# A block-sparse attention with two expert layers: four small edits of its first stage, and its hand-drawn order of work drawn up again

## The chip, the cores and the metric
One core of a Trainium2 chip runs the whole program; the other seven have no part in it. Times are device microseconds (us) of one execution. The time before is the median of three runs.

## What is computed
The reference, cut to what matters. Attention with a narrow window, and a summary of each 32 tokens as additional keys and values, then two dense layers:

```python
q, k, v: (2, 8, 768, 64)              # batch, heads, tokens, head width; float32
k_sum = k.reshape(B, H, 24, 32, D).max(axis=3)
v_sum = v.reshape(B, H, 24, 32, D).mean(axis=3)
scores_l = where(|pos_q - pos_k| < 16, scale * q @ k.T, -1e9)
scores_s = scale * q @ k_sum.T + log(32)
a = softmax(concatenate([scores_l, scores_s]))
x = a @ concatenate([v, v_sum])       # (1536 tokens, 512)
h = x @ moe_w_in                      # 512 -> 2048
x = (h * clip(h + 3, 0, 6) / 6) @ moe_w_out
h = x @ moe2_w_in
return (h * sigmoid(h)) @ moe2_w_out
```

## The kernel before, in words
The program is one list of some 1,960 named operations (`ORDER`, from line 111), which is walked through once. An entry is a function of the kernel with its numbers (`tr k 0 1 0` is `transposed("k", 0, 1, 0)`), and a star puts it on VectorE where it has a choice. Every engine takes its own instructions strictly in that order: PE (TensorE), DVE (VectorE), ACT (ScalarE), POOL (GpSimd), and SP (SyncE), on whose one queue all transfers are issued. So an instruction that waits holds up all that its engine has after it. Buffers and PSUM banks come from rings (`Ring`): `take` gives the buffer that has been free longest, `use` counts down its users. The compiled program has a wait wherever a buffer is taken again.

The stages. A batch has three blocks of 256 tokens for each of k, q and v. `load` (L458 and L473) brings a block in: keys of batch 0, and its first query block, as pairs of rows (512 B a piece), which `par` (by_parity, L486) sorts into even and odd tokens, one half on DVE, one on ACT; other k and q blocks come as two transfers with rows of 256 B straight into `raws`, a ring of two buffers in all. `tr` (L500) transposes half a block on PE in four matmuls; `k_copy` (L508) and `k_max` (L514) take keys and their block maxima out of the bank, `q_copy` (L527, L529) the queries. For each of 24 windows of 64 queries (a unit, numbered over both batches, 12 in each), `keys` (L591, L594) copies the 96 near keys and the 24 block maxima side by side; `scores` (L608) multiplies for two units at once, in 32 small matmuls; `masked` (L623) adds the mask and finds the row's maximum on DVE, `exps` (L637) are four exponentials on ACT, followed by `guard` (L648), `inverse` (L652) and `normal` (L657, on POOL or DVE); `turn` (L665) transposes the result and `turned` (L670) copies it out. `v_sums` (L545) sums values over 32 tokens on PE, each of the three blocks in its own bank; `v_add` (L556, L558) adds the three up in `vsum` on DVE, `v_rows` (L564) and `v_put` (L574) lay the sums beside the values that `load_v` (L581) brings per unit. `mix` (L679) multiplies two units with their values; `mixed_hi` and `mixed_lo` (L701, L705) split the result in two parts of reduced precision for the layers.

The layers: `fetch` (L416, L418) brings weights in 511 KB pieces into a ring of three (`words`), `conv_top`, `conv_join`, `conv_hi`, `conv_lo` (L426 to L450) split them into two parts; `hidden` (L721) is the first matmul of a step in 12 matmuls of 512 columns, in two halves, `project` (L798, L801) the second; the later part, from some 200 us on, goes by products of sums (`prod`, `prodb`, L1025). `warm` (L1173) and `rouse` (L1185) are groups of two matmuls on data that nobody uses, put where PE would wait.

## Time and profile before
| | |
|---|---|
| Median of three runs | 585.75 us (585.04 to 585.86) |
| The profiled execution, its own time | 585.98 us |
| Its span, from the first instruction to the last | 584.1 us |
| Mean granted TensorE clock | 1.00 |
| PE, DVE, ACT, POOL busy in the span | 97%, 79%, 46%, 16% |
| Bytes moved | 51.57 MB, mean 88 GB/s |

The shares are means over very different stages. In the first 60 us transfers, attention and the first weights run beside each other; later PE alone is full. A stage is read from its own stretch, and the engine that limits it from what its neighbours wait for. In a chain of waits each line is what ended last; a line of a transfer covers its issue, queueing and landing.

### The profile page before, as it was taken

To read this page: it belongs to the slowest core of one execution; us is meant where nothing else is said; L and a number is where in the kernel's file an instruction comes from. 1 tells how busy PE (TensorE), PEld (TensorE's weight loads), DVE (VectorE), ACT (ScalarE), POOL (GpSimd) and SP (SyncE) were. 2 spreads that over 40 slices of the span, in tenths; PEclk is the share of its full clock that TensorE was granted. 3 is DMA by queue.
4 is the path that set the end of the run, shared out by engine and by line. 5 is a ranking of instruction groups with operands and counts; after the bars stand their busy time and mean duration, and the time that the engine had idled before them with its cause. 6 is when DMAs were issued, how large, how long until landed. Compare 5 with 4: busy or idle time off the path is not lost.

```text
span 584.1 us, 9467 instructions
## 1 busy us (share of the span) xinstructions
PE 566.9 (97%) x3536; PEld 476.7 (82%) x3536; DVE 462.3 (79%) x1012; ACT 269.6 (46%) x626; POOL 95.8 (16%) x111
## 2 busy tenths in 40 slices
PE   6778999999999999999999999999999999999997
PEld 6667788888888788888888888888888898888886
DVE  4899888874776999998999999585877686757764
ACT  4798865542313345541646565545534234424220
POOL 1756252101010012121100202000100000111000
PEclk9999999999999999999999999999999999999999
DMA  9999982323010112333220110223122211210013
GB/s 239 258 191 261 214 202 87 100 64 98 0 38 0 51 57 73 109 89 119 80 71 3 37 37 30 79 77 125 50 73 83 98 37 36 73 66 8 1 71 146
DMA packets 69054, 51.57 MB, mean 88 GB/s; under 512 B 36368, under 2 KB 63504, under 8 KB 69008
## 3 DMA queue, kind: packets, MB, share of 16 engines
...
q14 instruction: 18, 0.15, 0.1%
...
## 4 chain that ended last, share of the span: by engine, by line
PE 88%; DVE 5%; DMA 3%; ACT 2%; issue 1%; SPq 0%; POOL 0%; DVEq 0%
PE bank L1025 29%; PE bank L801 22%; PE bank L798 20%; PE bank L721 11%; PE bank L679 2%; PE bank L665 1%; DMA stage<-in_v_dram 1%; PE bank L608 1%; DMA early_units<-in_v_dram 1%; ACT early_units L637 1%; DVE kmax L514 1%; DMA cst<-in_consts_dram 1%; PE bank L500 1%; DVE w L928 0%; DVE bits L435 0%
## 5 line engine op out<-in xcount | busy, mean ns | idle before, releaser
L801 PE MATMUL bank<-w,g 128*128 128x512 f32 (+1 forms) x477 | 111.7, 385 | 0.0
L798 PE MATMUL bank<-g,w 128*128 128x512 f32 x444 | 108.7, 391 | 0.4 <-DVE g L778 0.4
L801 PEld LDWEIGHTS bank<-w,g 128*128 128x128 f32 x477 | 88.2, 188 | 17.7
L450 POOL TENSOR_TENSOR w<-bits,w 128x512 fp32r<-128x512 f32 x34 | 47.9, 1411 | 304.0 <-ACT w L446 213.5
L798 PEld LDWEIGHTS bank<-g,w 128*128 128x128 f32 x444 | 82.5, 188 | 17.7 <-DVE g L778 0.8
L1025 PE MATMUL bank<-w,x 128*128 128x512 f32 (+1 forms) x360 | 73.9, 348 | 0.5 <-DVE w L971 0.5
L1025 PEld LDWEIGHTS bank<-w,x 128*128 128x128 f32 x360 | 59.4, 189 | 10.0 <-DVE w L971 0.8
L1025 PE MATMUL bank<-x,w 128*128 128x512 f32 (+1 forms) x240 | 49.6, 348 | 0.0
L426 ACT CAST top<-words 128x512 f16<-128x512 bf16 x51 | 39.7, 778 | 19.9 <-DVE bits L435 11.0
L721 PE MATMUL bank<-x,w 128*128 128x512 f32 x192 | 47.7, 396 | 0.0
L435 DVE SCALAR_TENSOR_TENSOR bits<-words,top 128x512 uint32<-128x512 uint32 x47 | 35.6, 756 | 14.0 <-ACT top L426 11.8
L1025 PEld LDWEIGHTS bank<-x,w 128*128 128x128 f32 x240 | 39.1, 189 | 5.5
L721 PEld LDWEIGHTS bank<-x,w 128*128 128x128 f32 x192 | 35.3, 188 | 7.8 <-issue 0.4
L778 DVE TENSOR_TENSOR g<-values,g 128x512 fp32r<-128x512 f32 x46 | 32.6, 712 | 7.4 <-ACT g L772 7.0
L752 ACT ACTIVATE values<-values 128x512 f32<-128x512 f32 x35 | 22.0, 628 | 29.3 <-DVE values L1066 17.0
L798 PE MATMUL bank<-w,w 128*128 128x512 f32 x132 | 33.6, 392 | 0.0
L752 ACT ACTIVATE r<-r 128x512 f32<-128x512 f32 x27 | 17.0, 629 | 28.9 <-DVE r L1072 20.0
L1072 DVE TENSOR_TENSOR values<-bank,values 128x512 f32<-128x512 f32 x39 | 26.5, 687 | 3.1 <-PE bank L1025 2.6
L798 PEld LDWEIGHTS bank<-w,w 128*128 128x128 f32 x132 | 24.5, 188 | 5.1 <-issue 0.2
L450 POOL TENSOR_TENSOR w<-cst,w 128x512 fp32r<-128x512 f32 x10 | 14.2, 1418 | 87.8 <-DVE w L446 60.6
L1025 PE MATMUL bank<-w,w 128*128 128x512 f32 (+1 forms) x144 | 28.1, 337 | 0.0
L772 ACT CAST g<-values 128x512 fp32r<-128x512 f32 x33 | 20.4, 621 | 16.7 <-PE bank L801 6.5
...
## 6 DMA issues: line engine op xcount, KB each, us to landing
...
out_dram<-acc SPq DMA_DIRECT2D x11, 256.0 KB, 2.0
early_w<-in_q_dram SPq DMA_DIRECT2D x10, 256.0 KB, 6.7
...
stage<-in_k_dram SPq DMA_DIRECT2D x3, 512.0 KB, 5.2
early_w<-in_k_dram SPq DMA_DIRECT2D x6, 256.0 KB, 6.2
stage<-in_v_dram SPq DMA_DIRECT2D x3, 512.0 KB, 7.5
```

The source lines that it names most:

```text
L426: copier("conv_top", h)(out=top[:, 1], in_=src[:, 2])
L435: nc.vector.scalar_tensor_tensor(out=bitss.take(h, bit_users(h)), in0=rest, scalar=13, in1=tops.use(h).bitcast(U32), op0=ALU.logical_shift ...
L450: eng.tensor_tensor(out=w_half(h, 1), in0=bitss.use(h).bitcast(F32), in1=w_half(h, 0).bitcast(F32), op=ALU.subtract,)
L679: nc.tensor.matmul(ps[D * e : D * e + D, o : o + QW], v[:NSLOT, h * D : (h + 1) * D], own(pTs, 2 * n + e)[:NSLOT, hp * P + QW * w : hp * P ...
L721: nc.tensor.matmul(ps[:, :n], w[:, a, kk * P : (kk + 1) * P], x[:, o // SUB : (o + n) // SUB, b, kk, :], start=(m == 0), stop=(m == last),)
L752: nc.scalar.activation(out=r, in_=ps, **kind)
L772: copier("gate_hi", i)(out=g[:, 0, cols], in_=value(i)[:, cols])
L778: eng.tensor_tensor(out=g[:, 1, cols], in0=r[:, cols], in1=g[:, 0, cols].bitcast(F32), op=ALU.subtract)
L798: nc.tensor.matmul(ps[:, o : o + n], lhs, g[:, b, shift : shift + n], **flags)
L801: nc.tensor.matmul(ps[:, : len(cols)], g[:, a, rows], rhs, **flags)
L1025: nc.tensor.matmul(ps, lhs(a, kk), rhs(b, kk), start=(i == 0), stop=(i == 5))
L1072: nc.vector.tensor_tensor(out=out, in0=banks.use(("prod", p, k)), in1=r, op=ALU.add)
```

## The change
Four edits in the code, and the first half of the list in another order. The order's last 957 entries are the same in both.

1. The first query block (`load q 0 0`) comes row by row, like the others, into `raws`; its two `par` entries are gone.
2. The value sums of a batch's three blocks accumulate in one bank, and `v_add` is one copy for the batch.
3. `scores 0` (units 0 and 1) reads near keys and maxima in place, in 64 matmuls, and `keys 0` and `keys 1` are gone.
4. There are twelve `rouse` groups where there were six.

In the list, `load v 1 0` goes behind the weights of the first layer steps, the first weights (`fetch 0`) and third query block (`load q 0 2`) behind values, and the first keys of batch 1 forward. Some 110 entries change between DVE and another engine. No work of the layers is added or left out.

```diff
+DIRECT = 1
...
-load k 0 1, zero, table 0, rouse 0, warm 6, load k 0 2, par k 1 0, load k 0 0, par k 1 1, par k 2 1, grow 9,
...
+zero, rouse 2, rouse 10, rouse 5, rouse 7, load k 0 0, par k 0 1, rouse 11, par k 0 0, table 0, clear,
...
-        if b == 0 and (what == "k" or T == 0):
+        if b == 0 and what == "k":
...
+    vdone = [0, 0]
...
-        ps = banks.take(("v", b, T), 1)
+        done = vdone[b]
+        vdone[b] += 1
+        if done == 0:
+            banks.take(("v", b), 1)
+        ps = banks.see(("v", b))
...
-                    start=(r == 0),
-                    stop=(r == 1 - b),
+                    start=(done == 0 and r == 0),
+                    stop=(done == 2 and r == 1 - b),
...
-    def v_add(b, T):
-        ps = banks.use(("v", b, T))
-        if T == 0:
-            nc.vector.tensor_copy(out=vsum, in_=ps[:, :P])
-        else:
-            nc.vector.tensor_tensor(out=vsum, in0=ps[:, :P], in1=vsum, op=ALU.add)
+    def v_add(b):
+        nc.vector.tensor_copy(out=vsum, in_=banks.use(("v", b))[:, :P])
...
-        kw = [own(kws, 2 * n + w) for w in range(2)]
+        if n < DIRECT:
+            near = [key_rows(b)[:, :, (t + w) * QW : (t + w) * QW + LOC] for w in range(2)]
+            pieces = [(0, near), (LOC, [kmax[b]] * 2)]
+        else:
+            pieces = [(0, [own(kws, 2 * n + w) for w in range(2)])]
```

Three places of the order, as the compiled programs have it. First, SP's queue from its start; a row is one transfer (or `x2`), `stage` and `early_w_88` are the buffers of pairs and of single rows, `128x8x128` are pieces of 512 B and `128x8x64` of 256 B. Before:

```order
L458 DMA stage_80<-in_k_dram 128x8x128
L1167 DMA cst<-in_consts_dram 128x176
L458 DMA stage_80<-in_k_dram 128x8x128
L458 DMA stage_81<-in_k_dram 128x8x128
L458 DMA stage_83<-in_q_dram 128x8x128
L473 DMA early_w_88<-in_k_dram 128x8x64 x2
L416 DMA words_69<-in_moe_w_in_dram 128x4x511
L1167 DMA cst<-in_consts_dram 128x360
L473 DMA early_w_88<-in_q_dram 128x8x64 x2
L458 DMA stage_84<-in_v_dram 128x8x128
L473 DMA early_w_88<-in_q_dram 128x8x64 x2
L458 DMA stage_84<-in_v_dram 128x8x128
```

And with the change:

```order
L459 DMA stage_80<-in_k_dram 128x8x128
L1178 DMA cst<-in_consts_dram 128x176
L474 DMA early_w_88<-in_q_dram 128x8x64 x2
L459 DMA stage_81<-in_k_dram 128x8x128
L474 DMA early_w_88<-in_k_dram 128x8x64 x2
L459 DMA stage_82<-in_k_dram 128x8x128
L1178 DMA cst<-in_consts_dram 128x360
L459 DMA stage_83<-in_v_dram 128x8x128 x2
L474 DMA early_w_88<-in_q_dram 128x8x64 x2
L459 DMA stage_84<-in_v_dram 128x8x128
L474 DMA early_w_88<-in_q_dram 128x8x64 x2
L417 DMA words_69<-in_moe_w_in_dram 128x4x511
```

The first queries moved ahead of two key blocks, and all three value blocks ahead of the third query block and of the weights.

Second, SP's queue further on, up to the second query block of batch 1, the last row of each piece; `early_units` and `early_r` with `96x8x64` or `80x8x64` are the values of single units. Before:

```order
L418 DMA words_70<-in_moe_w_out_dram 128x2047
L473 DMA early_w_88<-in_k_dram 128x8x64 x4
L581 DMA early_units<-in_v_dram 96x8x64
L581 DMA early_r_97<-in_v_dram 80x8x64
L581 DMA early_units<-in_v_dram 96x8x64
L458 DMA early_w_88<-in_v_dram 128x8x128
L581 DMA early_r_97<-in_v_dram 96x8x64
L473 DMA early_w_88<-in_q_dram 128x8x64 x2
L581 DMA early_units<-in_v_dram 96x8x64 x2
L581 DMA early_r_97<-in_v_dram 96x8x64 x2
L473 DMA early_w_88<-in_q_dram 128x8x64 x2
```

And with the change:

```order
L474 DMA early_w_88<-in_k_dram 128x8x64 x2
L584 DMA early_units<-in_v_dram 96x8x64 x2
L584 DMA early_r_97<-in_v_dram 96x8x64
L474 DMA early_w_88<-in_k_dram 128x8x64 x2
L419 DMA words_70<-in_moe_w_out_dram 128x2047
L584 DMA early_r_97<-in_v_dram 80x8x64
L474 DMA early_w_88<-in_q_dram 128x8x64 x2
L584 DMA early_units<-in_v_dram 96x8x64 x2
L584 DMA early_r_97<-in_v_dram 96x8x64 x2
L474 DMA early_w_88<-in_q_dram 128x8x64 x2
```

The 512 KB of `load v 1 0` (the row `early_w_88<-in_v_dram`) is no longer in this stretch, and the two key blocks of batch 1 stand apart.

Third, PE around its first `hidden` (`x_0_64` with a weight `w`); rows with `128x128 x4` are transposes, of queries (`early_w_88`) and of units (`120x128`). Before:

```order
L500 MATMUL bank_73<-cst,early_w_88 128x128 x4
L500 MATMUL bank_74<-cst,early_w_88 128x128 x4
L721 MATMUL bank_79<-x_0_64,w_87 128x512 x12
L665 MATMUL bank_77<-cst,early_w_95 120x128 x4
L665 MATMUL bank_74<-cst,early_w_95 120x128 x4
L721 MATMUL bank_73<-x_0_64,w_386 128x512 x12
```

And with the change:

```order
L676 MATMUL bank_76<-cst,early_w_95 120x128 x4
L501 MATMUL bank_79<-cst,early_w_88 128x128 x4
L732 MATMUL bank_75<-x_0_64,w_86 128x512 x6
L501 MATMUL bank_72<-cst,early_w_88 128x128 x4
L732 MATMUL bank_75<-x_0_64,w_86 128x512 x6
L676 MATMUL bank_76<-cst,early_units 120x128 x4
L676 MATMUL bank_79<-cst,early_w_95 120x128 x4
L732 MATMUL bank_74<-x_0_64,w_356 128x512 x12
```

One of the two query transposes went between the halves of the first `hidden`; a unit's transpose (`turn 8`) stands ahead of it now, and `turn 11` behind.

## Rows read from the trace of the kernel before

**Rows 1.** Page, part 1: busy us, share of the span and instructions of each engine.

```profile
PE 566.9 (97%) x3536; PEld 476.7 (82%) x3536; DVE 462.3 (79%) x1012; ACT 269.6 (46%) x626; POOL 95.8 (16%) x111
```

**Rows 2.** Busy us in stretches: PE, PEld, DVE, ACT, POOL; granted clock, DMA share, GB/s.

```profile
20.00:30.00 10.00, 7.82 (x134) 5.98 (x131) 7.64 (x31) 8.09 (x38) 6.03 (x7) 1.00 1.10 257
30.00:40.00 10.00, 7.35 (x116) 6.05 (x114) 9.56 (x53) 9.90 (x42) 4.74 (x9) 1.00 1.25 195
40.00:50.00 10.00, 9.07 (x205) 7.56 (x206) 8.28 (x29) 8.81 (x34) 6.69 (x12) 1.00 1.05 213
50.00:60.00 10.00, 8.79 (x74) 7.02 (x74) 9.79 (x35) 8.46 (x31) 6.08 (x7) 1.00 1.16 272
190.00:200.00 10.00, 9.61 (x45) 7.75 (x44) 9.73 (x19) 4.49 (x8) 0.45 (x1) 1.00 0.19 54
17.20:50.70 33.50, 27.10 (x500) 21.85 (x492) 28.98 (x139) 30.24 (x127) 20.04 (x35) 1.00 1.14 228
```

**Rows 3.** Timeline of PE: start, us, instruction, [idle before it, its releaser].

```profile
12.61 0.61 PE L1185 MATMUL bank<-early_w 128*128 128x128 f32 x4
...
29.79 0.65 PE L665 MATMUL bank<-cst,early_units 128*120 128x128 f32 x4
...
40.11 0.69 PE L679 MATMUL bank<-early_g,early_r 120*64 120x64 f32 x16 [0.54 <-DMA early_r<-in_v_dram]
...
49.85 1.09 PE L500 MATMUL bank<-cst,early_w 128*128 128x128 f32 x8
50.70 3.00 PE L721 MATMUL bank<-x,w 128*128 128x512 f32 x12
...
55.35 0.62 PE L665 MATMUL bank<-cst,early_w 128*120 128x128 f32 x4 [1.21 <-DVE early_w L657]
```

**Rows 4.** Chain of waits, from 0 to 60 us: start, us, what.

```profile
1.24 4.03 DMA cst<-in_consts_dram
...
7.38 2.57 PE bank L500 x12
...
11.61 3.00 DVE kmax L514 x5
...
17.20 1.63 ACT early_units L637 x8
...
19.12 7.52 DMA stage<-in_v_dram
...
46.74 0.98 PE bank L608 x32
```

**Rows 5.** Timeline of SP: start and us of the issue of a transfer.

```profile
30.74 0.67 SPq L581 DMA_DIRECT2D early_units<-in_v_dram  x1
31.78 0.66 SPq L458 DMA_DIRECT2D early_w<-in_v_dram  x1
32.49 1.95 SPq L581 DMA_DIRECT2D early_r<-in_v_dram  x1
...
42.87 2.24 SPq L473 DMA_DIRECT2D early_w<-in_q_dram  x2
```

**Rows 6.** Transfers from 4 to 8 us, nearly all in pieces of 512 B.

```profile
DMA packets 2308, 1.18 MB, mean 295 GB/s; under 512 B 51, under 2 KB 2308, under 8 KB 2308
```

**Rows 7.** Transfers from 28 to 32 us, all under 512 B; an issue's median us to landing.

```profile
DMA packets 3146, 0.79 MB, mean 198 GB/s; under 512 B 3146, under 2 KB 3146, under 8 KB 3146
...
early_w<-in_v_dram SPq DMA_DIRECT2D x1, 512.0 KB, 7.3
```

**Rows 8.** Issues from 40 to 44 us: KB each, median us to landing.

```profile
early_w<-in_q_dram SPq DMA_DIRECT2D x2, 256.0 KB, 5.3
```

**Rows 9.** Values of single units (L581), issues from 30 to 33 us.

```profile
DMA to landing us min/median/max: 6.0/6.0/7.6
```

**Rows 10.** Groups by line, 0 to 60 us: busy us, mean ns, idle before.

```profile
L591 POOL COPY early_units<-kT 128x384 f32<-128x384 f32 x8 | 4.1, 509 | 13.2 <-ACT kT L508 11.5 <-PE bank L608 1.7
L486 DVE COPY stage<-stage 128x512 f32<-128x512 f32 x4 | 1.7, 425 | 5.7 <-DMA stage<-in_k_dram 5.7
```

More of the change, by code (lines that the diff above doesn't have):

```diff
@@ L132 @@
-load_v 5, keys 12, exps 10, guard 10, tr q 1 0 0, inverse 10, q_copy 1 0 0, mixed_hi 1, turn 5, mixed_hi 0,
-masked 9, turned 5, turn 11, mixed_lo 1, mix 3, normal 10, turn 10, q_copy 1 0 1*, load q 1 1, keys 13,
-turned 11, mixed_hi 3*, mixed_lo 3, scores 6, fetch 2, turned 10, mixed_lo 0, keys 14, keys 15, mix 2,
-scores 7, mixed_hi 2*, mixed_lo 2, tr q 1 1 1, exps 8, guard 8, exps 9, masked 14, inverse 8, tr q 1 1 0,
-conv_top 2*, conv_join 2, guard 9, fetch 4, q_copy 1 1 0, hidden 0 0, q_copy 1 1 1, conv_top 4, hidden 0 1,
@@ new lines @@
+v_put 0 3, tr q 0 2 0, v_put 0 0, v_put 0 2, unstage, k_max 1 0 0, inverse 3, normal 3, q_copy 0 1 0*,
+load k 1 2, turn 3, load_v 2, inverse 2, normal 2*, inverse 1, normal 1, tr q 0 2 1, q_copy 0 2 1, scores 3,
+masked 7, load_v 3, keys 4*, guard 0, inverse 0, v_put 0 1, conv_top 0, conv_join 0, turned 3*, turn 1,
+load_v 1, turn 2, masked 6, turned 1*, scores 2, exps 7, guard 7, inverse 7, turned 2*, normal 0, turn 0,
+keys 9, turned 0, masked 4, exps 6, guard 6, inverse 6, q_copy 0 2 0, tr k 1 2 1, warm 6, k_copy 1 2 1*,
@@ new lines @@
+conv_hi 0*, load k 1 1, fetch 1, mix 1, keys 8, normal 7, mixed_hi 1, mixed_lo 1, exps 4, guard 4, load_v 0,
+keys 11, masked 5, exps 5, guard 5, tr k 1 2 0, k_max 1 2 1, normal 6, inverse 4, turn 6, load q 1 0, turn 7,
+turned 7, turned 6*, keys 10, normal 4, k_copy 1 2 0, scores 5, masked 10, tr k 1 1 1, exps 10, mix 0,
+k_max 1 1 1, k_copy 1 1 1*, inverse 5, conv_top 1*, conv_join 1, scores 4, masked 11, turn 4, guard 10,
+tr k 1 1 0, k_copy 1 1 0, normal 5, turn 5, tr q 1 0 1, masked 8, q_copy 1 0 1, load_v 6, inverse 10,
@@ new lines @@
+load_v 7, exps 8, normal 10*, turn 10, guard 8, k_max 1 2 0, turned 4*, k_max 1 1 0, inverse 8, keys 12,
+turned 5, keys 15*, masked 9, keys 14, mix 3, conv_hi 1*, grow 9, tr q 1 0 0, q_copy 1 0 0, keys 13,
+mixed_hi 0, mixed_lo 0, load_v 5, load_v 4, mix 2, normal 8, scores 7, mixed_hi 3, mixed_lo 3, load q 1 1,
+fetch 2, mixed_hi 2*, mixed_lo 2, scores 6, exps 11, turn 8, keys 17*, guard 11, conv_lo 0, inverse 11,
+masked 12, exps 9, guard 9, conv_top 2*, inverse 9, normal 11, turned 8, tr q 1 1 1, q_copy 1 1 1,
@@ new lines @@
+scores 8, masked 16, load_v 10, conv_lo 6, gate_hi 1, gate_lo 1, load_v 9, mix 4, act 2, hidden 3 0, exps 16,
+turned 12*, project 0 0, load v 1 0, conv_hi 3*, v_pair 1 0*, v_sums 1 0, conv_lo 3*, gate 2, gate_hi 2*,
+gate_lo 2, normal 13, turn 13, guard 16, turned 13, inverse 16, load_v 11, normal 16, masked 17, fetch 5,
+conv_top 5, conv_join 5, mixed_hi 4, load v 1 2, mixed_lo 4, exps 17, mix 5, mixed_hi 5, exps 14, guard 14,
+conv_hi 5, fetch 8, conv_top 8*, conv_join 8, conv_hi 8*, hidden 3 1, mixed_lo 5, project 1 0, load v 1 1,
@@ new lines @@
+gate 3, act 5, gate 5, conv_hi 9, turn 15, conv_lo 7, q_copy 1 2 0*, normal 17*, q_copy 1 2 1, project 2 1,
+turned 15, grow 1, turn 16, turn 17, turn 14, gate_hi 3*, keys 18, gate_hi 4*, load_v 13, gate_lo 3,
+gate_lo 4, turned 14, load_v 15, load_v 14, mix 6, turned 16, mix 7, fetch 12, turned 17*, scores 9, keys 20,
+keys 21, mixed_hi 6*, mixed_lo 6, mixed_hi 7, mixed_lo 7, fetch 11, project 3 0, conv_top 11, load_v 16,
+conv_join 11, conv_hi 11*, conv_lo 11*, project 3 1, conv_top 12, conv_join 12, conv_hi 12*, fetch 14,
@@ new lines @@
+conv_top 14, conv_lo 12*, hidden 8 0, conv_join 14, hidden 10 0, hidden 10 1, act 10, masked 18, masked 19,
+grow 0, load_v 17, fetch 15, hidden 8 1, conv_top 15, gate 10, gate_hi 5*, hidden 6 0, conv_hi 14, exps 19,
+guard 19, act 8, gate_lo 5, inverse 19, normal 19*, hidden 6 1, act 6, gate 6, project 5 0, mix 8, exps 18,
+gate 8, conv_lo 14*, conv_join 15, conv_lo 9, guard 18, inverse 18, mixed_hi 8, mixed_lo 8, fetch 16,
+scores 10, keys 23, project 4 0, fetch 13, normal 18, project 4 1, fetch 18, turn 18, turned 18, masked 20,
@@ new lines @@
+conv_top 13*, conv_join 13, hidden 9 0, gate_hi 6, turn 19, gate_lo 6, hidden 7 0, hidden 7 1, exps 20,
+guard 20, masked 21, conv_hi 13, conv_lo 13*, conv_hi 15*, exps 21, project 5 1, guard 21, load_v 18,
+conv_lo 15, act 7, gate 7, gate_hi 7, inverse 21, grow 5, conv_top 18*, project 6 0, hidden 11 0, turned 19*,
+conv_join 18, hidden 9 1, normal 21*, turn 21, project 6 1, gate_lo 7, project 7 0, load_v 19, act 9,
+finish 0 0 0 0, mix 9, gate 9, gate_hi 9*, load_v 20, keys 22*, scores 11, masked 23, exps 23, guard 23,
```

197 lines of the change are left out of this document (85 added, 112 removed).

## The prediction
> **What bounds the kernel now.** I read four views in this order. The busy times of the page first: TensorE (PE) is busy 566.9 us of a span of 584.1 [rows 1], so all that any order of work can win back is the time in which PE has nothing to do, 17.2 us, and the stretched matmuls beside it. Then the stretches of 10 us: from 20 to 60 us PE is busy 7.82, 7.35, 9.07 and 8.79 of each ten, and far behind that, at 190 to 200 us, there is a second, small dent of 0.39 [rows 2]. So the loss lies at the start, before the first expert layer runs. Third, PE's timeline: its first large matmul (`hidden 0 0`) starts at 50.70, and the next long wait, 1.21 us, is over at 55.35 [rows 3]. From there PE always has work. The time of the kernel is therefore, nearly, the moment at which `hidden 0 0` starts, plus the PE work still to be done then.
>
> What sets that moment is read from the chain of waits: a transfer of values (v, block 2 of batch 0) that lands at 19.12 + 7.52 = 26.64 carries the chain over 7.5 us, after ScalarE's (ACT) first exponentials at 17.20 [rows 4]. Two resources are nearly full all the way: the DMA engines (share 1.05 to 1.25 in the stretches from 20 to 60, 195 to 272 GB/s) and ACT, which is busy 30.24 of the 33.50 us from its first exponential to `hidden 0 0` [rows 2]. VectorE (DVE) has 28.98 there, GpSimd (POOL) 20.04. The last transfer ahead of `hidden 0 0` is the second query block of batch 1 (`load q 1 1`): issued at 42.87 and after, the later half landing some 5.3 us behind its issue, at about 49.0; its eight transposes begin at 49.85 and `hidden 0 0` is right behind them [rows 3, 5, 8].
>
> **The change, part by part.**
>
> *Queue of transfers.* Everything here runs on SP's one queue, so a transfer taken out ahead moves up all behind it. A transfer of 512 KB with rows of 512 B runs at 295 GB/s, 1.78 us; one with rows of 256 B at 198 GB/s, 2.65 us [rows 6, 7]. First the cost: the first queries now come row by row, 2.65 for 1.78, +0.87, and +0 is the other end, if small rows ran at the better rate. I take +0.87. The Trainium skill speaks against this edit too: its page "DMA: Bandwidth & Descriptors" (Specifications; Why small descriptors are slow) asks for at least 512 B and counts 27% overhead on 256 B. By its count (11 cycles for 256 B, and by the same formula 19 for 512) an estimate of the cost is +0.3, and the sum below would be 0.6 us lower; the row is the dearer and decides.
>
> Now the gains. Ahead of v block 2, the first weights (511 KB, 1.8 us at the better rate) and the third query block (2.65) are gone: 0.87 - 1.8 - 2.65 = -3.6, so it lands near 23.0 instead of 26.6. Ahead of `load q 1 1`, `load v 1 0` is gone, worth 1.78 by its rate, or 2.4 by the landings (31.78 + 7.3 = 39.1 against the transfer before it, 30.74 + 6.0 = 36.7) [rows 5, 7, 9]: with the +0.87 this is -0.9 to -1.5, landing 47.5 to 48.1. The value rows of `mix 0` also gain this: today its last ones land at 32.49 + 7.6 = 40.1, and PE waits 0.54 us for them [rows 3, 5, 9].
>
> *Order around the first `hidden`.* Only one of the two transposes of `load q 1 1` still stands ahead of it (four matmuls; eight take 0.85 from 49.85 to 50.70), so the landing at 47.5 to 48.1 allows 48.1 to 48.7: a gain of 2.0 to 2.6, and I take 2.3. One group of four transposes more than before then lies behind `hidden 0 0` (two moved behind it, one ahead): +0.43. Net **-1.9 us**.
>
> *Does ACT allow that?* The same twelve exponential units stand ahead of `hidden 0 0` in both orders. The first starts where the last key block lands: after the table at 1.24 + 4.03 = 5.27 come two transfers with small rows and two with large ones, 14.1; then a sorting copy (0.43), transposes (0.6), two maxima (0.6 each), scores and the mask's first step (0.5): 16.8, and 18.7 if three further maxima (five take 3.00) queue ahead on DVE, against 17.20 now [rows 4, 10]. So ACT starts 0.4 earlier to 1.5 later; it idles 33.50 - 30.24 = 3.26 us on its way now. If it idles not at all, it allows -1.8 to -3.7; the forecast needs most of that idle time to go. What speaks for it: the values land 3.6 us earlier.
>
> *Smaller edits.* Two query blocks lose their key copies (0.5 us and a little, on POOL and DVE, one each [rows 10]), DVE loses a 0.43 us sorting copy and two small adds of value sums, but takes five key copies where it had one. All of it lies on engines with room: POOL 20.04, DVE 28.98 of 33.50 [rows 2]; cost 0 on the path, up to +1 if DVE, the fuller, comes late. `scores 0` has 64 small matmuls for 32; 32 take 0.98 [rows 4]. The first half needs no maxima and runs while those are made, the other lies behind the last maximum for some tenths, counted above; ends 0 and +1.0, taken 0. Six warming groups are added, 0.61 each [rows 3]: in PE's waits nothing, all exposed 3.7. PE is idle 5.8 us from 20 to 50 [rows 2], so I take 0.
>
> *Behind 60 us* the same work is only dealt out anew among DVE, ACT and POOL. PE has one dent there, 0.39 in its stretch with DVE at 9.73 [rows 2]: gone or doubled, I take 0, ends -1 and +1. The wait of 1.21 at 55.35 for a DVE product (unit 9) I leave as it is; its end is -1.2.
>
> **Sum.** The profiled execution took 585.98, 0.23 above the median of 585.75. 585.98 - 1.9 = 584.1, or **583.9** in the terms of the median. The forecast's own spread is 582.7 to 584.8. A measurement of this kernel can tell some 0.2%, 1.2 us, from no change.
>
> **Rivals.**
> *More than forecast:* the value landing's whole 3.6 us is passed on and the 1.21 wait goes. 585.75 - 3.6 - 1.2 + 0.4 = 581.4; down to 580. For it: the chain runs over that landing. Against it: `load q 1 1` alone can't land before 47.5.
>
> *Nothing comes through:* the first exponential 1.5 later and ACT full gives -1.8; with half its idle time left, -0.2, and the transfers then no longer matter. 584.8 to 586.9. For it: ACT at 9.90 from 30 to 40 us. This is also the case that the redrawn order doesn't do what it claims: the transfers are as late as before, only for other work.
>
> *Slower, by a wait in the transfer queue:* row loads share two buffers. `load k 1 1` may be issued only when `tr q 0 2 1` has emptied one, and that stands on PE behind `turn 3`, which waits for a unit to be normalised. Today `turn 3` runs at 29.79, 3.2 us behind the values' landing at 26.64 [rows 3, 4]; with the landing at 23.0 that makes 26.2, and the buffer is free at 26.6 to 27. A landing at 32 to 33, where the rates put it, wants the issue 6 us before [rows 9], 26 to 27: there is no slack. Every microsecond beyond 27 delays the load, all behind it on SP (weights, values of `mix 0`, both query blocks), and `hidden 0 0`. If `turn 3` ran where it runs today, the buffer would come 3.4 late: -1.9 + 3.4 = +1.5, 587.3; with the warming groups exposed, 588 to 589. It decides from about 29 us on.
>
> *The clock:* PE's granted clock is 1.00, the 2.4 GHz level, in every stretch of rows 2; the early transposes ran at half pace (twelve in 2.57 us, 0.214 each, against 0.11 from 49.85) [rows 3, 4], directly after PE had waited for the table until 5.27. With new waits for keys the pace could fall again: ten groups of four at half pace are 40 x 0.11 = 4.3 us, half of it in waits: 583.9 + 2.2 = 586.1. The Trainium skill's "TensorE: Matmul & The Clock Gate" (HAM oscillation) states this rule, that PE drops to 1.2 GHz after idling; the trace agrees only in those early transposes.
>
> **Chances.** Forecast 0.45, more 0.15, nothing 0.19, slower 0.16, clock 0.05. Faster by over 0.2% (below 584.6): forecast and more, without its upper edge, 0.60; within 0.2%: 0.21 (nothing, most of the clock, that edge); slower, above 586.9: 0.19 (the queue, and upper ends of the others). The range 580.5 to 587.3 leaves out half of the slower case and the lowest end.
>
> **What would show it.** Right: v block 2 lands at 22 to 24, first exponential by 18.7, `load q 1 1` by 48.1, `hidden 0 0` at 48 to 49, no wait over 1.5 us on PE from there on, clock 1.00. Wrong: `hidden 0 0` at 50.5 or later; an SP wait at `load k 1 1` until 29 or more; PE dents in 60 to 270 us that add up to over 2 us; transposes at 0.21 us after 20 us.

## The result, and the profile after

The changed kernel takes 593.13 us (591.82 to 593.83); the kernel before, on the same chip, 585.81 (585.04 to 586.29). The ratio is 1.0124, 95% interval [1.0101, 1.0146]: slower by 7.3 us, where 583.9 and a gain of 1.9 was forecast. The time lies above the range.

Its profiled execution took 593.62, its span is 591.8, the mean clock 0.994. The busy times of the page, first part, beside [rows 1]:

```profile
PE 573.2 (97%) x3592; PEld 481.6 (81%) x3592; DVE 465.8 (79%) x1023; ACT 263.1 (44%) x616; POOL 92.1 (16%) x100
```

PE is busy 6.3 us longer for the same layers (573.2 for 566.9; 56 small matmuls more, and some that run at the lower clock), and idle 1.4 us longer. Where, the stretches tell; columns as in [rows 2]: PE, PEld, DVE, ACT, POOL busy, granted clock, DMA share, GB/s. After:

```profile
0.00:10.00 10.00, 7.07 (x40) 6.60 (x40) 0.90 (x3) 3.17 (x5) 1.46 (x10) 1.00 0.94 199
10.00:20.00 10.00, 6.80 (x125) 5.56 (x126) 6.54 (x16) 3.79 (x8) 1.43 (x4) 1.00 1.24 269
20.00:30.00 10.00, 9.15 (x142) 7.40 (x135) 7.60 (x42) 9.30 (x42) 2.70 (x4) 1.00 1.06 222
30.00:40.00 10.00, 7.62 (x132) 6.18 (x132) 9.33 (x47) 8.71 (x38) 6.32 (x12) 1.00 1.02 201
40.00:50.00 10.00, 7.80 (x120) 6.44 (x120) 9.93 (x47) 6.43 (x26) 4.42 (x8) 0.84 1.02 209
50.00:60.00 10.00, 10.00 (x138) 8.49 (x137) 8.42 (x30) 9.09 (x35) 6.54 (x6) 0.99 0.56 170
60.00:70.00 10.00, 9.61 (x97) 7.28 (x97) 9.86 (x38) 6.51 (x25) 5.96 (x6) 1.00 1.10 257
70.00:80.00 10.00, 7.95 (x63) 6.06 (x62) 9.86 (x22) 7.72 (x32) 4.89 (x5) 0.83 0.52 159
17.20:54.30 37.10, 30.67 (x561) 25.06 (x553) 31.68 (x146) 28.47 (x119) 16.75 (x28) 0.95 1.03 217
46.80:50.10 3.30, 3.30 (x40) 2.85 (x38) 3.28 (x15) 1.58 (x8) 1.73 (x5) 0.50 0.94 238
74.10:77.40 3.30, 3.30 (x26) 2.71 (x21) 3.30 (x13) 3.30 (x14) 2.55 (x2) 0.50 0.93 275
```

And four stretches of the kernel before that were not read for the prediction:

```profile
0.00:10.00 10.00, 5.91 (x26) 5.62 (x27) 2.11 (x6) 3.14 (x4) 1.46 (x10) 1.00 0.89 222
10.00:20.00 10.00, 8.03 (x125) 6.86 (x123) 9.76 (x39) 6.13 (x19) 4.93 (x14) 1.00 1.25 262
60.00:70.00 10.00, 10.00 (x114) 7.43 (x114) 9.79 (x37) 8.01 (x22) 3.94 (x4) 1.00 1.16 222
70.00:80.00 10.00, 10.00 (x84) 8.24 (x80) 6.80 (x23) 9.76 (x34) 4.98 (x6) 1.00 1.09 215
```

Three things stand in these rows. First, VectorE did 2.11 + 9.76 = 11.87 us of work in the first 20 us before, and does 0.90 + 6.54 = 7.44 now: 4.4 us less. Second, from 40 to 50 it is full (9.93), and the granted clock is at half, 1.2 GHz, for 3.4 us. Third, from 60 to 80 us, where PE had no gap at all, it is now idle for 0.39 + 2.05 us, beside a full VectorE, and the clock falls for 3.4 us a second time.

The timeline of PE after (start, us, instruction, [idle before it, its releaser]) beside [rows 3]:

```profile
18.76 0.66 PE L619 MATMUL bank<-kmax,early_w 64*64 64x24 f32 x32 [0.89 <-DVE kmax L515]
...
43.55 0.65 PE L676 MATMUL bank<-cst,early_w 128*120 128x128 f32 x4 [0.46 <-POOL early_w L668]
44.91 0.66 PE L501 MATMUL bank<-cst,early_w 128*128 128x128 f32 x4 [0.71 <-DVE stat L634]
46.59 0.96 PE L676 MATMUL bank<-cst,early_units 128*120 128x128 f32 x4 [1.03 <-ACT early_w L648]
47.48 1.98 PE L690 MATMUL bank<-early_units 120*64 120x64 f32 x32
...
54.30 1.62 PE L732 MATMUL bank<-x,w 128*128 128x512 f32 x6
...
72.28 0.43 PE L552 MATMUL bank<-early_w,cst 128*32 128x128 f32 x8 [1.85 <-DVE early_w L537]
```

And VectorE and GpSimd just ahead of the first of these waits, then VectorE's same step, the join of weight block 1, in the kernel before:

```profile
42.73 1.32 DVE L436 SCALAR_TENSOR_TENSOR bits<-words,top 128x512 uint32<-128x512 uint32 x1
...
42.42 1.08 POOL L668 TENSOR_TENSOR early_w<-early_w,stat 128x480 f32<-128x480 f32 x1 [1.61 <-DVE stat L663]
```

```profile
31.52 0.69 DVE L435 SCALAR_TENSOR_TENSOR bits<-words,top 128x512 uint32<-128x512 uint32 x1
```

`hidden 0 0` starts at 54.30, not 50.70 as before or 48 to 49 as forecast. Three waits between 43 and 47 us add up to 2.20 (0.54 + 0.20 in the same place before), and then the clock is at half from 46.73 to 50.14, which makes 1.7 us of PE work last 3.4 (the same 32 matmuls of a `mix` take 1.98 at 47.48 and 1.15 at full pace). Behind `hidden 0 0`, the wait of 1.21 at 55 us is gone (PE is busy 10.00 from 50 to 60), but the new gaps of 60 to 80 us cost 0.39 + 2.05, and the second fall of the clock 1.7. From 100 to 300 us PE's idle time goes from 0.89 to 1.34. The sum is 3.6 - 1.2 + 2.4 + 1.7 + 0.5 = 7.0 of the 7.7 us between the spans; of the 0.7 left, the group of transposes that the prediction counted behind `hidden 0 0` would be 0.43; the rest is not traced.

The transfers came nearly as forecast. SP's timeline and the issues from 16.0 to 16.5 and from 42.9 to 44.5 us (KB each, median us to landing), beside [rows 4, 5, 8]:

```profile
16.03 1.64 SPq L459 DMA_DIRECT2D stage<-in_v_dram  x1
...
43.01 1.51 SPq L474 DMA_DIRECT2D early_w<-in_q_dram  x2
...
stage<-in_v_dram SPq DMA_DIRECT2D x1, 512.0 KB, 7.6
...
early_w<-in_q_dram SPq DMA_DIRECT2D x2, 256.0 KB, 4.7
```

v block 2 landed at 16.03 + 7.6 = 23.6 (forecast 23.0, before 26.6), the later half of `load q 1 1`, issued at 43.62, at 48.1 to 48.4 (forecast 47.5 to 48.1). So the part of the sum that was worked out with most care nearly held, and the time went the other way. PE's waits ahead of `hidden 0 0` are no longer for transfers. The first of the three is put down to GpSimd's `normal`, which had itself waited 1.61 us for VectorE (above), the second is for VectorE's masks, the third is put down to ScalarE's exponentials, though what PE transposes there comes out of VectorE's `normal` at 45.79, behind the same masks. That VectorE is the cause was therefore likely, and had to be tested.

### The profile page after: what moved, and what is told of

Read it like the earlier page. It is cut to its first block, busy times and chain, and to the rows that moved or that the text cites. A ratio compares the mean times of both kernels' runs of the same rounds, so it can differ in the third digit from the quotient of the medians.

```text
span 591.8 us, 9566 instructions
## 1 busy us (share of the span) xinstructions
PE 573.2 (97%) x3592; PEld 481.6 (81%) x3592; DVE 465.8 (79%) x1023; ACT 263.1 (44%) x616; POOL 92.1 (16%) x100
## 4 chain that ended last, share of the span: by engine, by line
PE 84%; DVE 9%; DMA 2%; ACT 1%; issue 1%; SPq 1%; POOL 0%; DVEq 0%
PE bank L1036 29%; PE bank L812 22%; PE bank L809 20%; PE bank L732 8%; PE bank L690 2%; DMA stage<-in_v_dram 1%; PE bank L676 1%; PE bank L501 1%; DMA early_w<-in_k_dram 1%; DVE top L427 1%; DVE bits L436 1%; PE bank L619 1%; DVE early_units L634 1%; DVE values L774 1%; DVE values L927 1%
## 5 line engine op out<-in xcount | busy, mean ns | idle before, releaser
L809 PE MATMUL bank<-g,w 128*128 128x512 f32 x432 | 106.1, 392 | 0.0
L809 PEld LDWEIGHTS bank<-g,w 128*128 128x128 f32 x432 | 80.2, 188 | 17.3 <-issue 0.5
L451 POOL TENSOR_TENSOR w<-bits,w 128x512 fp32r<-128x512 f32 x30 | 42.9, 1431 | 301.6 <-ACT w L447 220.3
L732 PE MATMUL bank<-x,w 128*128 128x512 f32 x192 | 49.1, 405 | 0.4 <-DVE stat L634 0.4
L427 ACT CAST top<-words 128x512 f16<-128x512 bf16 x48 | 37.4, 780 | 25.8 <-DVE bits L436 13.9
L809 PE MATMUL bank<-w,w 128*128 128x512 f32 x144 | 36.7, 391 | 0.8 <-DVE w L789 0.8
L809 PEld LDWEIGHTS bank<-w,w 128*128 128x128 f32 x144 | 26.8, 188 | 6.6 <-DVE w L789 1.2
L1036 PE MATMUL bank<-w,w 128*128 128x256 f32 (+1 forms) x144 | 28.4, 336 | 0.0
L1083 DVE TENSOR_TENSOR r<-bank,r 128x512 f32<-128x512 f32 x29 | 19.8, 688 | 10.1 <-PE bank L1036 9.9
L789 DVE TENSOR_TENSOR g<-r,g 128x512 fp32r<-128x512 f32 x31 | 21.2, 687 | 7.7 <-ACT g L783 7.3
```

What stands on the lines that cost most here:

```text
L427: copier("conv_top", h)(out=top[:, 1], in_=src[:, 2])
L451: eng.tensor_tensor(out=w_half(h, 1), in0=bitss.use(h).bitcast(F32), in1=w_half(h, 0).bitcast(F32), op=ALU.subtract,)
L732: nc.tensor.matmul(ps[:, :n], w[:, a, kk * P : (kk + 1) * P], x[:, o // SUB : (o + n) // SUB, b, kk, :], start=(m == 0), stop=(m == last),)
L789: eng.tensor_tensor(out=g[:, 1, cols], in0=r[:, cols], in1=g[:, 0, cols].bitcast(F32), op=ALU.subtract)
L809: nc.tensor.matmul(ps[:, o : o + n], lhs, g[:, b, shift : shift + n], **flags)
L1036: nc.tensor.matmul(ps, lhs(a, kk), rhs(b, kk), start=(i == 0), stop=(i == 5))
```

## The experiments

The diffs of the order show its entries and not its wrapped lines, with `...` for what is left out. Each time is followed by its ratio to the kernel before on the same chip, with the ratio's 95% interval; two experiments are compared by these ratios, since the chips differ. Starts and waits are those of one profiled execution.

### Which part costs what: the edits, the head of the order, the rest

`edits_alone` and `edits_alone2` have the four edits of the code in the old order, without the six added warming groups. In the second, the copy of the sums stands where the last `v_add` stood; in the first, right ahead of `v_rows`. (Both load the first queries row by row; the expectation of the second says otherwise, wrongly.)

```diff
-load q 0 0 (pairs), par q 0 1, par q 0 0, keys 1*, keys 0, v_add 0 0, v_add 0 1, v_add 0 2
+load q 0 0 (row by row), v_add 0
```

> The four edits in the order of before (first queries row by row, one bank for value sums, scores 0 in place; six warming groups as before). Theory 'order': the loss of 7.3 us comes from the new order, so this stays within 1 us of before, 585 to 587. Rival 'edits': the row-wise first queries and the 32 added matmuls delay the start, since the first scores of the changed kernel are made some 2 us later than before; then 587.5 to 588.5.

> The four edits of the code alone (first queries row by row is the table's and stays out; value sums in one bank, keys of two blocks in place, added sums as one step), in the order of the kernel before, the value sums added up where before's last one stood. Theory 'order' (all of the loss comes from the new order, the edits are worth nothing): within 1 us of the kernel before, no PE wait over 1 us behind 60 us that before does not have. Rival 'edits' (the wider sums and the keys in place are dearer by themselves): 588.5 or more, as in the first run of the edits alone, with a PE wait at the value rows again.

Measured: 589.88, 1.0064 [1.0042, 1.0087], and 587.51, 1.0025 [1.0015, 1.0035]. The first has a wait of 1.56 us at the `v_rows` of batch 1 that the second has not: the place of one copy of 0.28 us on VectorE was worth 0.4%. The clean price of the four edits is the second, 1.5 us.

`new_head` takes the changed order through `hidden 0 1` and the old one behind it, `new_tail` the reverse.

> The changed kernel's order up to and with hidden 0 1, then the entries that are left in the order of before. Theory 'two places' (hidden 0 0 is 3.6 us late, and a second stall of 4 us follows at 70 us in the new tail): the head alone costs 3 to 4, so 588.8 to 589.8. Rival 'all in the tail' (what the head loses is slack that a good tail takes up): 585 to 586.5. Rival 'all from the head': 592 to 593.5.

> The order of before up to and with hidden 0 1, then the changed kernel's order. Theory 'two places': the stall at 70 us, value pair late on VectorE and then TensorE at half clock, stays: 589 to 590. Rival 'all from the head': 585 to 586.5, since VectorE comes to that place in time.

Measured: `new_head` 594.27, 1.0128 [1.0109, 1.0147]; its tail has the ill-placed copy of `edits_alone` too, so the head alone is 1.0128 - 1.0064 = 0.64%, 3.7 us. `new_tail` 590.54, 1.0060 [1.0043, 1.0077], against `edits_alone2` 0.35%, 2.0 us. The three prices, 0.25 + 0.64 + 0.35, make 1.24%, which is what the whole change costs; with intervals of 0.1 to 0.3 on each, that they meet so exactly is luck, but no large part is missing. `new_head` shows the changed kernel's three waits again (0.46, 0.71, 1.03), with `hidden 0 0` at 54.30.

The edits were then parted again, in the old order: `q_rows_alone` has only the row-by-row first queries, `sums_keys_alone` only the others.

```diff
-        if b == 0 and (what == "k" or T == 0):
+        if b == 0 and what == "k":
```

> The kernel before with one edit: the first queries come row by row (two transfers of 1.68 us on the queue where one was, and the two copies that took the rows apart are gone). Theory 'the small rows are the price of the edits': +1.0 to +2.0 us, as for all four edits in the old order (+1.65), with the first value block landing 1.2 to 1.9 us later than 19.34. Rival 'the price is in the value sums or the keys': within 0.6 us of the kernel before.

> The kernel before with the other edits (value sums in one bank and added once, keys of two query blocks in place), its first queries loaded as before. Theory 'the small rows are the price': within 0.6 us of the kernel before, or up to 1 us faster (four additions and four key copies less). Rival 'the price is in the sums or the keys': +1.0 to +2.0 us, with a longer stretch of scores 0 (64 matmuls where 32 were) to be seen on the path to the first exponentials.

Measured: 586.82, 1.0018 [1.0009, 1.0027], +1.05 us, and 586.44, 1.0008 [0.9999, 1.0017], +0.5, not told apart from none. SP's timeline shows the first one's price: two issues of the small rows occupy the queue 3.45 us, where the one in pairs took 1.68, and two of keys behind it 2.77 for 3.52, together 1.0 us more. Before:

```profile
3.44 1.68 SPq L458 DMA_DIRECT2D stage<-in_q_dram  x1
5.17 3.52 SPq L473 DMA_DIRECT2D early_w<-in_k_dram  x2
...
12.46 2.43 SPq L458 DMA_DIRECT2D stage<-in_v_dram  x1
```

With rows:

```profile
3.48 3.45 SPq L466 DMA_DIRECT2D early_w<-in_q_dram  x2
6.97 2.77 SPq L466 DMA_DIRECT2D early_w<-in_k_dram  x2
...
13.75 1.78 SPq L451 DMA_DIRECT2D stage<-in_v_dram  x1
```

The first value block lands at 13.75 + 6.4 = 20.1 for 12.46 + 6.9 = 19.4: +0.8, near the +0.87 that the prediction took from the rates. The expectation's lower end for the landing, +1.2, was missed.

### The head: what makes `hidden 0 0` late

`old_start` takes the old order through `scores 0`, so that all keys of batch 0 come first again, and the changed one from there.

```diff
-load q 0 0, tr q 0 0 1, load k 0 2, ..., load k 1 0, ..., load k 0 1, ..., scores 0
+load k 0 1, ..., load k 0 2, ..., load k 0 0, ..., load q 0 0, ..., load k 1 0, ..., fetch 0, ..., scores 0
```

> Before's order through the first scores (all keys of batch 0 ahead of the second query part and of k 1 0), then the changed order. Theory 'late keys starve VectorE' (VectorE was busy 6.54 of the ten us from 10 to 20 instead of 9.76, and is full from 30 on): the 10 to 20 window is back over 9.3, hidden 0 0 starts 2 to 4 us earlier than in the changed kernel, and the time falls by 2 to 4 us against it. Rival 'VectorE is over-loaded later anyway' (weights ahead of the masks): time and hidden 0 0 within 1 us of the changed kernel.

Measured: 593.11, 1.0117 [1.0097, 1.0138]: nothing gained, `hidden 0 0` at 55.50. VectorE came to 2.13 + 7.32 us in the first 20 us, half of what it had lost, and then waited in two other places (VectorE's timeline, the two longest waits):

```profile
18.25 0.28 DVE L627 CUSTOM_DVE_ANT_0 early_w<-bank,cst 128x120 f32<-128x120 f32 x1 [2.15 <-PE bank L612]
...
24.02 0.69 DVE L521 TENSOR_SCALAR early_w<-bank 128x512 f32<-128x512 f32 x1 [2.26 <-PE bank L494]
```

In the kernel before, the conversion of the first weights stood in these places (0.46 us at 16.17, 1.46 and 0.43 from 21.99), which the changed order puts off. So `old_start_fill` puts that back as well:

```diff
 scores 0
+conv_top 0*, conv_join 0
...
+conv_hi 0*
 q_copy 0 1 1*
...
-conv_top 0, conv_join 0, ..., conv_hi 0*
```

> The run with the old start (keys first, then the changed order, 593.11), and the conversion of weight block 0 (top, join, high half; some 1.5 us of VectorE) put back into VectorE's idle time right behind the first scores, where the old order had it. Theory 'VectorE idle early is what is missing later': hidden 0 0 comes 1 to 1.5 us earlier than 55.50 there, the time falls by 0.7 to 1.5. Rival 'what stands right ahead of hidden 0 0 sets it, early idle time is harmless': within 0.5 us.

Measured: `hidden 0 0` at 52.26, 3.2 us earlier than in `old_start`, more than expected; the time 592.36, 1.0113 [1.0080, 1.0147], not told apart from it. What came back at `hidden 0 0` did not come back at the end.

`join_later` and `weights_later` take weight conversions from ahead of `hidden 0 0`: the first one only as far as `mix 3`, the second behind `hidden 0 0`.

```diff
-inverse 5, conv_top 1*, conv_join 1, scores 4, masked 11
+inverse 5, scores 4, masked 11
...
-mix 3, conv_hi 1*, ..., conv_top 2*, ..., conv_join 2, hidden 0 0
+mix 3, ..., hidden 0 0, conv_top 2*, conv_join 2
...
+conv_top 1*, conv_join 1, conv_hi 1*, conv_lo 1
```

(In `join_later` the two entries stand ahead of `conv_hi 1*` in its old place, and block 2 stays.)

> The changed kernel with the top and joining of weight block 1 (0.43 + 1.32 us of VectorE) taken from ahead of scores 4 and masked 11 to just ahead of its next step, behind mix 3. Theory 'weight work stands ahead of the masks': PE's waits between 43 and 47 us (0.46, 0.71, 1.03) lose over half, hidden 0 0 comes 1.5 us or more earlier, and the granted clock may stay at 1.00 there, worth another 1.7. Rival 'VectorE is full': the wait only moves, hidden 0 0 and the time within 0.7 us.

> The changed kernel with the conversion of weight blocks 1 and 2 (some 2.3 us of VectorE) put behind hidden 0 0 instead of ahead of it. Theory 'VectorE is the bound of the head': hidden 0 0 comes 1.5 to 2.3 us earlier; the end gains as much or less, since hidden 1 0 and project 0 0 then wait for their weights. Rival 'one block's chain is the bound': hidden 0 0 within 0.7 us, and the end the same or later.

Measured: `join_later` 593.96, 1.0130 [1.0110, 1.0151]. Of the three waits one is gone and two shrank (0.37 and 0.32 are left), and the clock stays at 1.00 there; but a wait of 2.08 us for VectorE's `mixed_lo` came at 53.80 in their place, and one of 0.75 for ScalarE at 55.72: the rival was right (28.58 us from `v_rows 0` to `hidden 0 0`; see the table below). `weights_later` 591.65, 1.0098 [1.0081, 1.0115]: `hidden 0 0` comes at 51.80, 2.5 us earlier, as VectorE's relief by 2.3 us foretold, and the time falls by some 1.5, by intervals that overlap (the changed kernel has 1.0124 [1.0101, 1.0146]). The rest went behind it (PE's timeline and the stretch from 60 to 70):

```profile
51.80 1.62 PE L725 MATMUL bank<-x,w 128*128 128x512 f32 x6
...
60.34 0.73 PE L725 MATMUL bank<-x,w 128*128 128x512 f32 x2 [1.45 <-DVE stat L627]
62.31 3.83 PE L725 MATMUL bank<-x,w 128*128 128x512 f32 x10 [1.23 <-POOL w L444]
...
60.00:70.00 10.00, 8.43 (x85) 6.44 (x86) 9.90 (x33) 6.18 (x25) 6.88 (x7) 0.83 1.15 247
```

`dve_relief` gives eight copies ahead of `hidden 0 0` from VectorE to ScalarE instead.

```diff
-q_copy 0 1 0*, turned 1*, turned 2*, turned 6*, k_copy 1 1 1*, conv_top 1*, conv_hi 1*, mixed_hi 2*
+q_copy 0 1 0, turned 1, turned 2, turned 6, k_copy 1 1 1, conv_top 1, conv_hi 1, mixed_hi 2
```

> The changed kernel with eight copies ahead of hidden 0 0 taken from VectorE to ScalarE (one query copy, three of turned, one key copy, top and high half of weight block 1, one mixed half; some 4.3 us of VectorE, 3.5 to 4 us of ScalarE, which has 8.6 us free between 17.2 and 54.3). Theory 'VectorE is the bound of the head': hidden 0 0 comes 2 to 4 us earlier than 54.30 and the time falls by 1.5 to 4 us against the changed kernel. Rival 'the chain of one block (mask, exponentials, normal, turn, mix) is the bound, whoever copies': hidden 0 0 within 1 us, or later.

Measured: 594.58, 1.0148 [1.0133, 1.0164]; `hidden 0 0` at 55.82. VectorE was relieved (6.50 us of work from 40 to 50 instead of 9.93), yet waited 3.46 us at 45.24 for ScalarE's `conv_top 1`, which stood in ScalarE's own queue behind exponentials. What one engine is spared, it may lose waiting for the other. Since the copy's place in the order was kept, this run does not test its theory: it neither clears nor convicts VectorE.

`both_fixes` joins `old_start_fill` and `weights_later`.

> The changed order with both remedies: keys first and weight block 0 converted right behind the first scores (as in old_start_fill, hidden 0 0 at 52.26 there), and weight blocks 1 and 2 converted behind hidden 0 0 (as in weights_later, 51.80 there). Theory 'VectorE's total work sets both stops': hidden 0 0 near 50 (between 49.5 and 51), but VectorE is still over 9.8 of each ten us from 60 to 80, so the end gains less: 590 to 591.5. Rival 'hidden 0 0 carries the end': the time falls by as much as hidden 0 0 comes earlier, to 588.5 to 589.5.

Measured: 592.79, 1.0095 [1.0079, 1.0111]; `hidden 0 0` at 52.05, not near 50. PE's timeline:

```profile
27.79 1.06 PE L560 MATMUL bank<-early_w,cst 128*32 128x128 f32 x8 [0.38 <-DVE early_w L554]
...
52.05 1.62 PE L725 MATMUL bank<-x,w 128*128 128x512 f32 x6
```

By the start of `hidden 0 0` alone, the two remedies do not add up. But a profile shows one execution, and its start varies: up to `mix 0` the order of `both_fixes` is that of `old_start_fill`, and yet its first value rows (`v_rows 0`, the first line) come 1.34 us later, with a granted clock of 0.83 from 20 to 30 us. So the stretch from `v_rows 0` to `hidden 0 0` is the better measure, and the time from there to the end of the span beside it (us; the last two columns are differences of starts and spans):

| | `v_rows 0` | `hidden 0 0` | between | to the end |
|---|---|---|---|---|
| before | 27.82 | 50.70 | 22.88 | 533.4 |
| `edits_alone` (old order, ill-placed copy) | 28.09 | 50.83 | 22.74 | 536.5 |
| `new_tail` (old head) | 28.20 | 51.16 | 22.96 | 536.6 |
| changed | 25.80 | 54.30 | 28.50 | 537.5 |
| `new_head` (old tail, ill-placed copy) | 26.07 | 54.30 | 28.23 | 538.3 |
| `pair_pool` (changed head) | 27.29 | 56.78 | 29.49 | 536.3 |
| `old_start` | 26.85 | 55.50 | 28.65 | 536.4 |
| `old_start_fill` | 26.45 | 52.26 | 25.81 | 537.5 |
| `weights_later` | 26.37 | 51.80 | 25.43 | 538.2 |
| `both_fixes` | 27.79 | 52.05 | 24.26 | 538.9 |

The changed order reaches the value rows 2.0 us earlier and then takes 5.6 us longer to `hidden 0 0`. Of these 5.6, putting the first conversions back early brings 2.8 (against `old_start`), taking the second ones behind `hidden 0 0` brings 3.1, and both bring 4.2. So most of the late head is the conversion of weights on VectorE, at the place where it now stands; for the 1.4 left, PE waits for a mask, a copy of VectorE's and GpSimd's `normal` (the longest, 1.04 at 38.64), and which of them counts stays open. The last column says why the time hardly follows: with the new order behind it, every kernel needs 536 to 539 us from `hidden 0 0` on, where the one before needs 533.4, and the three that start it earlier need 537.5 to 538.9 and so lose again a part of what they had gained. The late head itself seems to cost something there too: in these profiles `new_head` needs 1.8 us more than `edits_alone`, which has the same tail.

The clock and the warming groups. `more_rouse` adds eight groups in the places where the clock falls, `no_rouse` takes the six added ones out.

```diff
+rouse 12, turn 5, ..., rouse 13, tr q 1 0 1, ..., rouse 14, rouse 15, turn 10, ..., rouse 16 to rouse 19, v_sums 1 0
```
```diff
-rouse 10, ..., rouse 7, ..., rouse 11, ..., rouse 8, ..., rouse 6, ..., rouse 9
```

> The changed kernel with eight more groups of dummy matmuls, ahead of turn 5, tr q 1 0 1, turn 10 (2) and the first value sums of batch 1 (4), where PE waits and the clock then falls to 1.2 GHz (46.7 to 50.1 and 74.0 to 77.5 us). Theory 'the clock carries half of the loss': the granted clock stays at 1.00 in both stretches and the time falls by 1.5 to 3 us. Rival 'the waits carry it' (VectorE comes no earlier, PE only waits longer): the time within 0.7 us, or slower by the dummies' own time.

> The changed kernel without the six added warming groups (6 of 12 left). Theory 'they are worth nothing': within 1 us of the changed kernel, the clock at 1.2 GHz a few us longer in the first 12 us, as before. Rival 'they hold the clock in the head': slower by 1.5 us or more.

Measured: `more_rouse` 592.31, 1.0104 [1.0088, 1.0121]. The clock stays at 1.00 in both stretches, and `hidden 0 0` still comes at 55.41; its start was late here (clock 0.72 from 10 to 20), but from `v_rows 0` on it takes 28.23 us for 28.50. The time is 0.8 us under the changed kernel's, within the intervals. `no_rouse` 592.92, 1.0104 [1.0078, 1.0131], the same. So the fall of the clock comes behind the waits, and no cost of its own is seen: with it prevented, PE waits or warms instead. The intervals still leave room for nearly 3 us. `old_start` agrees, with the clock at 1.00 throughout and no less time.

### The second loss, at 72 us

In the changed order the first value block of batch 1 is loaded behind `hidden 0 0`, and its pair sum stands on VectorE, at 71.55 us. `pair_pool` gives the pair sum to GpSimd; `v1_early` also puts the load far ahead in the order.

```diff
-load v 1 0, conv_hi 3*, v_pair 1 0*, v_sums 1 0
+load v 1 0, conv_hi 3*, v_pair 1 0, v_sums 1 0
```
```diff
 tr k 1 1 0
+load v 1 0
...
 keys 13
+v_pair 1 0
...
-load v 1 0, conv_hi 3*, v_pair 1 0*, v_sums 1 0
+conv_hi 3*, v_sums 1 0
```

> The changed kernel with one entry altered: v_pair 1 0 on GpSimd, which is idle there, and not on VectorE. TensorE waited 1.85 us for it at 70.4 and then ran at half clock from 74.0 to 77.5 (1.7 us lost). Theory 'stall': both go, 593.1 - 3.5 = 589.6. Theory 'wait alone': the wait goes and the low clock stays, 591.3. Rival 'VectorE full': TensorE waits for VectorE's next product at the same place, 592.3 to 593.3.

> The changed kernel with the first value block of batch 1 loaded right behind tr k 1 1 0 (some 25 us earlier) and its pair sum on GpSimd behind keys 13 instead of on VectorE in the full stretch at 71 us. Theory 'moving this block behind hidden 0 0 made the second loss': PE's wait of 1.85 us at 72 and the fall of the clock behind it go, time 2 to 4 us less; hidden 0 0 0 to 1 us later by the transfer. Rival 'VectorE is full there anyway' (as with the pair sum on GpSimd alone): a wait for VectorE's turned and gate steps of 1.5 us or more takes its place, the time within 1 us.

Measured: `pair_pool` 592.62, 1.0105 [1.0080, 1.0129]; `v1_early` 596.39, 1.0165 [1.0138, 1.0192]. In `pair_pool` the wait of 1.85 is gone, and two others have its place (PE's timeline, then the stretch from 70 to 80):

```profile
73.88 0.62 PE L669 MATMUL bank<-cst,early_w 128*120 128x128 f32 x4 [0.98 <-DVE early_g L674]
75.44 1.15 PE L683 MATMUL bank<-early_units 120*64 120x64 f32 x32 [0.94 <-DVE values L767]
...
70.00:80.00 10.00, 8.08 (x70) 6.26 (x70) 9.86 (x31) 7.67 (x29) 5.78 (x5) 1.00 0.58 167
```

VectorE is as full as before, and whatever it does next is late. In `v1_early` the load was issued 15 us earlier (43.76 for 58.81), after it had waited 5.2 us in SP's queue for a buffer that PE had still to empty, with all other transfers behind it (SP's waits, then its timeline):

```profile
SPq L452 <- PE bank L494: 5.2, 1, 5.2
...
43.76 0.37 SPq L452 DMA_DIRECT2D early_w<-in_v_dram  x1
...
52.24 1.01 SPq L467 DMA_DIRECT2D early_w<-in_q_dram  x2
```

The values of `mix` came late, for which PE then waits 1.48 us at 49.34, `load q 1 1` went out at 52.24 for 43.01, the clock fell (0.66 from 50 to 60), and `hidden 0 0` starts at 58.08. So this run does not test its theory cleanly; it has the same two waits behind 75 us (0.69, 0.94). `new_tail`, with the old head and the clock at 1.00 all through, has them as well (0.53 at 68.55, 0.94 at 70.12, 0.47 at 78.84). So they belong to the order behind `hidden 0 1`, and not to the late head. Which entries of that order make VectorE late there was not found.

### Looking for a version that beats both

`sums_keys_alone` starts `hidden 0 0` at 50.09, 0.6 us earlier than the kernel before. On top of it `normal8_dve` takes one step off GpSimd, since VectorE's join of a weight block takes 1.32 us beside it.

```diff
-inverse 8, tr q 1 1 0, ..., normal 9*, normal 8, turn 8
+inverse 8, normal 8*, tr q 1 1 0, ..., normal 9*, turn 8
```

> The kernel before with the sums and keys edits, and normal 8 on VectorE (0.66 us) instead of GpSimd (1.07 us), so that VectorE's join of weight block 2 does not run beside it (1.32 us there, 0.69 alone). Theory: normal 9 ends 0.7 to 1.0 us earlier, PE's wait of 1.25 us at 54.78 shrinks to under 0.5, the time falls by 0.6 to 1.0 us against the run without it and lies 0 to 0.2% under the kernel before. Rival: GpSimd's low half of weight block 2 then runs beside normal 9 all the same, and hidden 1 0 waits for that: within 0.3 us of the run without it.

Measured: 586.07 beside 586.70, 0.9991 [0.9980, 1.0002]: at the edge, not shown to be faster. The join was quicker (VectorE's timeline):

```profile
51.86 0.69 DVE L429 SCALAR_TENSOR_TENSOR bits<-words,top 128x512 uint32<-128x512 uint32 x1
...
53.13 1.74 DVE L661 TENSOR_TENSOR early_w<-early_w,stat 128x480 f32<-128x480 f32 x1
```

but `normal 9` now met GpSimd's next step (1.26 us from 53.10) and took 1.74 where it takes 0.66 alone; PE's wait stayed (1.31 at 55.02). The rival was right. Nothing here beats the kernel before by more than the measurement can tell.

A further variant, the old order with `turn 9` put behind `hidden 1 0`, no longer computes the reference's function, and its time says nothing here.

## Why the prediction was wrong, step by step

*The queue of transfers* was nearly right: v block 2 at 23.6 for 23.0, `load q 1 1` at 48.1 to 48.4 for 47.5 to 48.1, the row-by-row queries +0.8 at the landing for +0.87 (in the old order). The Trainium skill's count ("DMA: Bandwidth & Descriptors", Why small descriptors are slow), by which an estimate of +0.3 was made, is below what the runs show. And the last key block landed at 13.8 (forecast 14.1). But the gain of 2.3 was booked on `load q 1 1`, and nothing waited for that transfer: the row of its transposes at 49.85 has no wait ahead of it [rows 3], and PE has none from 45.2 to 50.70. Its later half had been there for some 0.85 us in the kernel before; in the changed one its transposes run at 53.70 and 55.75, over 5 us behind the landing.

*The first exponentials* were put at 16.8 to 18.7. They came at 19.81 (VectorE's timeline, then ScalarE's):

```profile
15.02 3.68 DVE L515 TENSOR_REDUCE kmax<-bank 128x16 f32<-128x512 f32 x6 [0.73 <-ACT kT L509]
...
19.81 0.39 ACT L648 ACTIVATE early_w<-early_w,stat 128x120 f32<-128x120 f32 x1 [2.94 <-DVE stat L634]
```

Six maxima of the late key blocks, not five, run on VectorE to 18.7, and PE waits 0.89 for them before the second half of `scores 0` can start: 1.1 us beyond the dear end, by work that all comes at once when the keys come last.

*The step that failed* is the one of the smaller edits: "All of it lies on engines with room: POOL 20.04, DVE 28.98 of 33.50 [rows 2]; cost 0 on the path, up to +1 if DVE, the fuller, comes late." VectorE's room was read from 17.2 us on, as a sum. In the 20 us from the start it had done 11.87 us of work, nearly without a gap from 10 us on, and the changed order took 4.4 us of that away: 2.1 us are masks (2.61 before, 0.52 now), which come later with the last keys; 1.0 are a sorting copy and a key copy that the edits drop; 0.5 is the first step of the first weights. The sum up to `hidden 0 0` even fell, from 38.0 us to 37.1, but 31.68 us of it now lie behind 17.2 us, for 28.98. The gain was booked where transfers were moved back (the first weights and the third query block, behind values: -3.6), and the conversions that go with those weights were booked nowhere. In both kernels VectorE converts two weight blocks ahead of `hidden 0 0`, some 3.9 us; before, between 16 and 33 us, now between 31 and 50. The join of block 1 ran at 31.52 (0.69 us) and now runs at 42.73, beside a step of GpSimd, for 1.32, ahead of the masks for which PE waits at 44.91. `old_start_fill` and `weights_later` show what that costs: moving the conversions out of the way brings back 2.8 and 3.1 us between `v_rows 0` and `hidden 0 0`, both together 4.2 of 5.6. So the term that was put at 0, at most +1, measured 4.2 us of that stretch; the 1.4 left stay open.

*The premise* failed too, that the time is nearly the start of `hidden 0 0` plus the PE work behind it. `old_start_fill`, `weights_later` and `both_fixes` start it 2.0 to 2.5 us earlier than the changed kernel, and the end comes 0.6 to 1.7 us earlier by the ratios, at the edge of what can be told.

*"Does ACT allow that?"* was the right kind of question, put to the wrong engine. ScalarE has 8.6 us idle from 17.2 us to `hidden 0 0` now (28.47 busy of 37.10); in that stretch it has less to do than before, and VectorE more.

*The clock* was a rival with 0.05. It did fall, in two places, each time for 3.4 us directly behind PE waits (2.20 us in three between 43 and 47; 1.85 in one). As a cause of its own it is not shown: with the clock held up by dummy work, the time fell by no more than can be measured.

*Behind 60 us* ±1 was given, and +4.1 came (0.39 + 2.05 of waits, 1.7 by the clock); in `new_tail` by itself, with no fall of the clock, the price is 2.0. `load v 1 0` was counted as a gain for being out of the way ahead of `load q 1 1`. The pair sum, the value sums and the copies that depend on it went with it into 60 to 80 us, where VectorE had 9.79 of ten from 60 to 70 already. Only the slower rival's sign was right; its mechanism, a wait in SP's queue at `load k 1 1`, hardly came: that load was issued at 29.14, beyond the 27 that it was said to need, but right behind the issues ahead of it; only its second half waited 0.6 us for a buffer. The block landed near 35.5, and no one waited for it: its first transpose stands on PE at 39.35. The mechanism itself is real, as `v1_early` shows with its 5.2 us.

*Warming groups* at 0: right.
